# Softmax denominators turned by TensorE, four operand sets in the first unit, finished keys kept in DRAM

## The chip, the cores and the metric

One core of a Trainium2 chip runs the kernel. The metric is the device time of one execution in microseconds (us), median of several runs. TensorE (PE), VectorE (DVE), ScalarE (ACT), GpSimd (POOL) and the queue that issues DMAs (SP) each run their own instruction stream in order.

## The reference

Two batches of eight heads, 768 tokens, head size 64. Each query attends to the keys of its own hash bucket (six sign bits of a projection); then come two feed-forward layers over 1536 tokens, all in fp32:

```python
q_bits = (np.einsum('bhsd,dk->bhsk', q, proj) > 0)      # likewise k_bits; a bucket is the six bits
scores = np.where(q_bucket == k_bucket, q @ k.T / 8, -1e9)
attn = exp(scores - max); attn = attn / (attn.sum(-1) + 1e-9)
x = (attn @ v)                                           # as (1536 tokens, 512)
h = x @ w_in;  x = (s * relu(h)**2 + b) @ w_out          # layer 1: 512 -> 2048 -> 512
h = x @ w_in2; out = (h * clip(h + 3, 0, 6) / 6) @ w_out2  # layer 2
```

## The kernel before

The tokens are cut into four units (two batches, two halves of 384 queries). Attention of a unit goes over four head pairs; pair `g` has six score tiles (two heads, three times 128 queries). A tile is: scores on PE (`qk`, L403), maximum on DVE (`smax`, L409), exponential with its row sum on ACT (`sexp`, L419), six 128x128 transposes on PE (`turn`, L425) and an eviction to SBUF by DVE or ACT (`evict`, L438 and L440). After six tiles `pv_mm` (L462) multiplies with the values. fp32 accuracy comes from splitting operands in a high and a low fp32r part (`k_hi`, `k_lo`, `q_hi`, `q_lo`, L332 to L354); the bucket masks are made by `bits_mm`, `bits`, `code_mm` and `buckets` (L368 to L391) and ride in the low part's other 64 rows.

The row sums stand one per partition, but the product `pv` has the queries along its free axis. So `recip` inverts the six columns, `r_store` (L449) writes them to DRAM element by element, `r_in` (L453) reads them back spread over the partitions as tile `R`, and DVE multiplies (`x_scale`, L467). `x_hi` and `x_lo` split the result for the feed-forward.

The feed-forward is eight jobs (`JOBS`): layer and unit, each 32 weight tiles with 12 matmuls (`mm`, L550), 384 in all. The jobs of units 0 and 1 come first, both layers; the score tiles of the later units are placed between the matmuls. The weights come as 64-bit floats: each tile is loaded (`w_load`, L486), its exponent rebased on ACT (`w_exp`, L494), two 16-bit pieces made (`w_ends`: DVE L503, POOL L506 for the sign and L508 for the rest), joined on DVE (`w_join`, L512), stored (L518), and fetched again by later jobs (`w_fetch`, L522). `w_hi` (ACT) and `w_lo` (POOL, L533) split every weight tile of every job.

The order of all engines is written out ahead of time by a planner (`Plan`): each operation has durations per engine, a due time, operations that it needs, and buffers that it takes and frees. It picks, engine by engine, the one that can start and is due first; where several engines can do an operation, the one that ends it first. The engines then run these lists in order, whatever really happens. The plan holds for the two DMAs of the denominators these lines:

```python
add("DMA", a + 4.0, (0.45, 0.34), r_store, (g,), needs=[("rc", g)], gives=[("rs", g)])
add("DMA", a + 6.5, (0.62, 0.55), r_in, (g,), needs=[("rs", g)], acq=[("R", ("R", g))], gives=[("R", g)])
```

The functions that the change touches:

Of the kernel before, what the change touches and what calls it, by code (L numbers as in the profile page):

```python
# [19 lines left out]
S = 768  # L20
# [8 lines left out]
WARM = 12  # L29
# [5 lines left out]
class Plan:  # L35
# [7 lines left out]

    EPS = {"PE": 0, "ACT": 0.15, "DVE": 0.3, "POOL": 0.15, "SP": 0.3}
# [81 lines left out]
    def forward(self, due):  # L126
# [13 lines left out]
        while left:  # L140
            able = {}
            for o in ready:
# [9 lines left out]
                else:  # L152
                    pick = None
                    for eng, dur in o[0].items():
# [72 lines left out]
def attn_moe_moe2(ctx, tc, qT, kT, vN, cst, w1_in, w1_out, w2_in, w2_out, out):  # L227
# [45 lines left out]
    rden = [dr_p.tile([6, 128], F32, name=f"rd{g}") for g in range(NP)]  # L273
# [6 lines left out]
    def first_unit():  # L280
        p = fab.enter_context(tc.tile_pool(name="first", bufs=1, side="right"))
        K.append([p.tile([128, 2, S], F32R, name=f"K{a}x") for a in range(2)])
        op["kx"] = p
        op["ptx"] = fab.enter_context(tc.tile_pool(name="ptx", bufs=2, side="right"))
        ps["Sx"] = xab.enter_context(tc.tile_pool(name="ps_x", bufs=1, space=PSUM))

    def later_units():
        fab.close()
        p = ctx.enter_context(tc.tile_pool(name="g", bufs=1, side="right"))
        G.extend(p.tile([128, 2, NQ], F32R, name=f"G{f}") for f in range(16))  # L290

# [4 lines left out]
    def keys(g):  # L296
        return K[g % 2 if g < 4 else 0]
# [6 lines left out]

    def load_k(g):
        u, hp = pairs[g]
        if g in (1, 3):
            t = op["kx"].tile([128, 2, S], F32, tag="krx", name="krx")
        else:
            t = one_p.tile([128, 2, S], F32, tag="kr", name="kr")  # L310
        queue[0].dma_start(out=t, in_=kT[units[u][0], hp])
        pd[g]["k"] = t

    def load_q(g):
        u, hp = pairs[g]
# [69 lines left out]
    def buckets(g, nm, h):  # L385
        t = pd[g][nm + "h"][64:128].rearrange("p (i n) -> p i n", i=2)[:, :, 0:384]
        if nm == "k":
            dst = keys(g)[1][64:128, h].rearrange("p (i n) -> p i n", i=2)
            nc.vector.tensor_scalar(out=dst, in0=t, scalar1=cnt, scalar2=-BIG, op0=ALU.not_equal, op1=ALU.mult)
        else:  # L390
            nc.vector.tensor_scalar(out=Q[g % 2][1][64:128], in0=t, scalar1=cnt, scalar2=None, op0=ALU.is_equal)  # L391
# [104 lines left out]
    def w_ends(key, half, on):  # L496
# [8 lines left out]
        elif half:  # L505
            nc.gpsimd.tensor_scalar(out=f16, in0=r16, scalar1=32768.0, scalar2=32768.0, op0=ALU.is_ge, op1=ALU.mult)  # L506
        else:
            nc.gpsimd.tensor_scalar(out=f16, in0=r16, scalar1=2.0 ** -13, scalar2=2.0 ** -14 - 0.5, op0=ALU.mult, op1=ALU.add)  # L508
# [97 lines left out]
    plan = Plan({"S": 2, "Sx": 1, "pv": 1, "mm": 1, "mmx": 2, "P": 2, "pt": 2, "ptx": 2, "v": 2, "R": 1,  # L606
# [31 lines left out]
    add("POOL", A[SPU - 1] + 0.1, 0.0, later_units, (), needs=[("pv", g) for g in range(4)], gives=["G"])  # L638
    for g in range(NP):
# [3 lines left out]
        old = {0: [], 1: [], 2: [0], 3: [1], 4: [2]}.get(g, [g - 1] if g < 9 else [g - 2, g - 1])  # L643
        kfree = [("qk", SPP * x + i) for x in old for i in range(SPP)]
        qfree = [("qk", SPP * (g - 2) + i) for i in range(SPP)] if g > 1 else []
        x = "x" if g in (1, 3) else ""
        St = ("S", "Sx") if g < 4 else "S"
        if own:
            add("DMA", t, (0.62, 2.2), load_k, (g,), acq=[("kr" + x, ("kr", g))], gives=[("k", g)])
            add({"ACT": 1.45, "POOL": 3.0, "DVE": 1.0}, t, 0, k_hi, (g,), needs=kfree + [("k", g)], gives=[("kh", g)], rel=[(("kr", g), 3)])  # L650
            add({"POOL": 3.5, "DVE": 1.7}, t, 0, k_lo, (g,), needs=[("kh", g)], gives=[("kl", g)], rel=[(("kr", g), 3)])
        add("DMA", t, (0.62, 1.1), load_q, (g,), acq=[("qr" + x, ("qr", g))], gives=[("q", g)])
        add({"ACT": 0.75, "POOL": 1.6, "DVE": 0.6}, t, 0, q_hi, (g,), needs=qfree + [("q", g)], gives=[("qh", g)], rel=[(("qr", g), 4)])
        add({"ACT": 0.75, "POOL": 1.6, "DVE": 0.6}, t, 0, q_top, (g,), needs=qfree + [("q", g)], gives=[("qt", g)], rel=[(("qr", g), 4)])
        add({"POOL": 2.9, "DVE": 0.95}, t, 0, q_lo, (g,), needs=[("qh", g)], gives=[("ql", g)], rel=[(("qr", g), 4)])
        for nm in ("kq" if own else "q"):
# [12 lines left out]
        if own or g % 2 == 0 or g < 8:
            pass  # L670
        add("DMA", t + 4, (0.45, 1.1), load_v, (g,), acq=[("v", ("v", g))], gives=[("v", g)])
        for i in range(SPP):
# [4 lines left out]
            add("PE", a, 0.69, qk, (s,), needs=[("kh", gk), ("kl", gk), ("kB", gk, h), ("qt", g), ("ql", g), ("qB", g)] + gate(s) + ([("qk", s - 1)] if s else []),  # L677
                acq=[(St, ("S", s))], gives=[("qk", s)])
            add("DVE", a + 1.0, 0.95, smax, (s,), needs=[("qk", s)], gives=[("mx", s)])
            add("ACT", a + 2.3, 1.17, sexp, (s,), needs=[("mx", s)] + ([("ex", s - 1)] if i else []), acq=[("P", ("P", s))], gives=[("ex", s)])  # L680
            add("PE", a + 3.6, 0.6, turn, (s,), needs=[("ex", s)], gives=[("tr", s)], rel=[(("P", s),)])
            add({"ACT": 0.85, "DVE": 0.85}, a + 4.4, 0, evict, (s,), needs=[("tr", s)] + ([("pt", s - 1)] if tq else []),
                acq=[(("pt", "ptx") if g < 4 else "pt", ("pt", g, h))] if tq == 0 else [], gives=[("pt", s)], rel=[(("S", s),)])
        for c in range(NC):
            add("PE", a + 6.0, 0.64, pv_mm, (g, c),
                needs=[("pv", g, c - 1)] if c else [("pt", SPP * g + i) for i in range(SPP)] + [("v", g)],
                acq=[] if c else [("pv", ("pv", g))], gives=[("pv", g, c) if c < 5 else ("pv", g)],
                rel=[(("pt", g, 0),), (("pt", g, 1),), (("v", g),)] if c == 5 else [])
        add("DVE", a + 3.6, 0.4, recip, (g,), needs=[("ex", SPP * g + i) for i in range(SPP)], gives=[("rc", g)])
        add("DMA", a + 4.0, (0.45, 0.34), r_store, (g,), needs=[("rc", g)], gives=[("rs", g)])  # L690
        add("DMA", a + 6.5, (0.62, 0.55), r_in, (g,), needs=[("rs", g)], acq=[("R", ("R", g))], gives=[("R", g)])
        add("DVE", a + 10.4, 0.6, x_scale, (g,), needs=[("R", g), ("pv", g)], gives=[("xs", g)], rel=[(("R", g),)])
        add("ACT", a + 11.0, 0.48, x_hi, (g,), needs=[("xs", g)], gives=[("xh", g)])
# [121 lines left out]
```

## Time and profile before

| | |
|---|---|
| median of 3 runs | 999.42 us (998.89 to 1007.68) |
| the profiled execution | 1008.91 us, span 1007.1 us |
| busy share of the span | PE 86%, DVE 48%, ACT 49%, POOL 55% |
| matmuls' granted clock, mean | 0.924 |
| DMA | 130.09 MB, mean 129 GB/s |

Busy time is when an engine executes; the ends of matmuls are modelled, so a busy PE is not PE at its peak. The clock is a share of 2.4 GHz. The chain of waits follows the work that ended last back to the start; its shares sum to the span. The profiled execution stands 0.95% above the median; sums are made against it.

### The profile page before, as it was taken

The numbers are of one execution on the slowest core, as the hardware profiler recorded it, in microseconds if no ns is written. First come the engines' busy times: TensorE is split into PE (matmuls) and PEld (weight loads), VectorE is DVE, ScalarE is ACT, GpSimd is POOL, SyncE is SP. The second block draws the span as 40 slices with busy tenths as digits, with TensorE's granted clock in tenths as the row PEclk, the third lists the DMA queues.
The fourth block names the chain that finished last, engine by engine and source line by source line (L and its number), as shares of the span: only waits on it lengthen the run. The fifth ranks groups of instructions, "written<-read, shape, count | busy, mean of one in ns | idle before, by whom it ended". The sixth has DMA issues, their size and how long they took to land.

```text
span 1007.1 us, 13158 instructions
## 1 busy us (share of the span) xinstructions
PE 865.7 (86%) x4668; PEld 718.0 (71%) x4668; DVE 484.8 (48%) x662; ACT 490.1 (49%) x899; POOL 556.9 (55%) x383
## 2 busy tenths in 40 slices
PE   8845569697877999889689889798899899999998
PEld 3523346566465999768466757656799699999998
DVE  6744337576644535788364556243352252250330
ACT  4623246555432654666344646333464374473652
POOL 6733008598665557997664233232364256666664
PEclk7977979899898899999698999898999999999999
DMA  8422324356574347555593355242343244445442
GB/s 300 131 56 55 92 66 157 103 183 145 179 158 109 108 162 231 181 180 166 188 190 97 103 123 86 76 61 79 104 132 95 61 121 131 124 127 149 134 136 85
DMA packets 71601, 130.09 MB, mean 129 GB/s; under 512 B 18672, under 2 KB 26992, under 8 KB 71536
## 3 DMA queue, kind: packets, MB, share of 16 engines
q1 hardware_dynamic: 71392, 129.05, 45.7%
q8 instruction: 36, 0.59, 0.3%
q14 instruction: 29, 0.24, 0.1%
q10 hardware_dynamic: 144, 0.22, 0.1%
HBM read 109.27 MB, written 19.97 MB: 128 GB/s over the span
## 4 chain that ended last, share of the span: by engine, by line
PE 47%; DMA 32%; DVE 8%; POOL 8%; issue 3%; ACT 1%; SPq 1%; DVEq 0%; POOLq 0%; ACTq 0%
PE mm L550 39%; DMA rd<-rs 15%; DMA R<-rd 9%; DMA wr<-w_out 5%; POOL wf L506 4%; PE S L403 3%; PE S L425 2%; DVE wf L512 2%; PE S L368 1%; POOL wl L533 1%; DVE nx L409 1%; POOL wf L508 1%; DMA wr<-w_in 1%; DMA qr<-q_t 1%; PE pv L462 1%
## 5 line engine op out<-in xcount | busy, mean ns | idle before, releaser
L533 POOL TENSOR_TENSOR wl<-wf,wh 128x512 fp32r<-128x512 f32 x256 | 335.9, 1314 | 321.4 <-ACT wh L527 317.9
L550 PE MATMUL mm<-X,wh 128*128 128x384 f32 x1024 | 277.8, 352 | 24.5 <-ACT X L471 19.3
L550 PE MATMUL mm<-G,wh 128*128 128x384 f32 x1024 | 280.1, 355 | 0.0
L527 ACT CAST wh<-wf 128x512 fp32r<-128x512 f32 x256 | 157.8, 617 | 146.7 <-PE mm L550 87.4
L550 PEld LDWEIGHTS mm<-X,wh 128*128 128x128 f32 x1024 | 187.3, 195 | 45.7 <-ACT X L471 20.5
L550 PEld LDWEIGHTS mm<-G,wh 128*128 128x128 f32 x1024 | 185.6, 196 | 33.3 <-issue 30.0
L550 PE MATMUL mm<-G,wl 128*128 128x384 f32 x512 | 177.0, 346 | 7.1 <-POOL wl L533 7.1
L550 PE MATMUL mm<-X,wl 128*128 128x384 f32 x512 | 176.6, 345 | 1.3 <-POOL wl L533 1.3
L403 PE MATMUL S<-K,Q 128*128 128x512 f32 x336 | 82.1, 369 | 49.1 <-DVE ptx L440 24.3
L409 DVE TENSOR_REDUCE nx<-S 128x1 f32<-128x768 f32 x96 | 91.5, 954 | 51.3 <-PE S L403 50.7
L419 ACT ACTIVATE P<-S,nx 128x768 f32<-128x768 f32 x96 | 86.6, 902 | 45.4 <-DVE nx L409 42.5
L550 PEld LDWEIGHTS mm<-G,wl 128*128 128x128 f32 x512 | 100.1, 196 | 8.6 <-POOL wl L533 8.6
L403 PEld LDWEIGHTS S<-K,Q 128*128 128x128 f32 x336 | 58.5, 204 | 66.2 <-DVE pt L440 21.6
L425 PE MATMUL S<-cv,P 128*128 128x128 f32 x576 | 89.5, 298 | 18.8 <-ACT P L419 18.8
L506 POOL TENSOR_SCALAR wf<-wr 128x512 uint16<-128x512 uint16 x45 | 100.7, 2244 | 6.4 <-ACT wr L494 3.3
L425 PEld LDWEIGHTS S<-cv,P 128*128 128x128 f32 x576 | 74.2, 154 | 39.4 <-ACT P L419 23.5
L550 PEld LDWEIGHTS mm<-X,wl 128*128 128x128 f32 x512 | 100.0, 195 | 1.6 <-POOL wl L533 1.6
L512 DVE SCALAR_TENSOR_TENSOR wf<-wr,wf 128x512 int32<-128x512 int32 x64 | 69.7, 1089 | 46.0 <-POOL wf L506 44.8
L508 POOL TENSOR_SCALAR wf<-wr 128x512 uint16<-128x512 uint16 x49 | 47.6, 971 | 60.9 <-DMA wr<-w_out 34.2
L467 DVE TENSOR_TENSOR pv<-pv,R 128x384 f32<-128x384 f32 x16 | 9.0, 566 | 144.1 <-DMA R<-rd 144.1
L494 ACT ACTIVATE wr<-wr 128x512 f32<-128x512 f32 x64 | 43.1, 675 | 68.0 <-DMA wr<-w_out 54.8
L462 PE MATMUL pv<-pt,v 128*64 128x384 f32 x336 | 71.4, 509 | 0.0
(330 smaller groups left out, 777.3 us busy)
## 6 DMA issues: line engine op xcount, KB each, us to landing
wf<-w SPq DMA_DIRECT2D x192, 256.0 KB, 2.7
wr<-w_in SPq DMA_DIRECT2D x32, 512.0 KB, 4.3
w<-wf SPq DMA_DIRECT2D x64, 256.0 KB, 5.6
wr<-w_out SPq DMA_DIRECT2D x32, 512.0 KB, 4.1
kr<-k_t SPq DMA_DIRECT2D x10, 768.0 KB, 4.4
qr<-q_t SPq DMA_DIRECT2D x16, 384.0 KB, 3.9
v<-v_n SPq DMA_DIRECT2D x16, 384.0 KB, 6.8
R<-rd SPq DMA_DIRECT2D x16, 192.0 KB
```

Of the source, the lines that this page charges most:

```text
L403: nc.tensor.matmul(out=sp[:, c0:c1], lhsT=Q[g % 2][a][:, h, 128 * t:128 * t + 128], rhs=keys(g)[a][:, h, c0:c1], start=(a == 0), stop=(a = ...
L409: nc.vector.reduce_max(out=nx, in_=sd[s]["sp"][:, 0:S], axis=AX.X, negate=True)
L419: nc.scalar.activation(out=d["p"], in_=d["sp"][:, 0:S], func=AF.Exp, bias=d["nx"], scale=1.0, accum_out=pd[g]["sums"][:, c:c + 1])
L425: nc.tensor.transpose(d["sp"][:, 128 * c:128 * c + 128], d["p"][:, 128 * c:128 * c + 128], ident)
L462: nc.tensor.matmul(out=d["pv"][64 * h:64 * h + 64, 0:NQ], lhsT=d["v"][:, c, 64 * h:64 * h + 64], rhs=d[h][:, c, :], start=(c == 0), stop=( ...
L494: nc.scalar.activation(out=a, in_=a, func=AF.Copy, scale=2.0 ** -112)
L506: nc.gpsimd.tensor_scalar(out=f16, in0=r16, scalar1=32768.0, scalar2=32768.0, op0=ALU.is_ge, op1=ALU.mult)
L508: nc.gpsimd.tensor_scalar(out=f16, in0=r16, scalar1=2.0 ** -13, scalar2=2.0 ** -14 - 0.5, op0=ALU.mult, op1=ALU.add)
L512: nc.vector.scalar_tensor_tensor(out=wf, in0=wq[key]["raw"][:, :, 1], scalar=3, in1=wf, op0=ALU.logical_shift_left, op1=ALU.bitwise_or)
L527: nc.scalar.copy(hi.rearrange("p a b -> p (a b)"), wq[key]["wf"])
L533: nc.gpsimd.tensor_tensor(out=lo.rearrange("p a b -> p (a b)"), in0=d["wf"], in1=d["hi"].rearrange("p a b -> p (a b)").bitcast(F32), op=AL ...
L550: nc.tensor.matmul(out=a, lhsT=w[:, k, :], rhs=src[k][:, xi, :], start=(k0 + k == 0 and p == 0), stop=(k0 + k == nk - 1 and p == 2))
```

## The change

The denominators no longer go over DRAM. `widen` copies the inverted sums to 64 columns each, `spread` turns the three 128x128 blocks by transposes on PE into PSUM, `r_copy` takes them to SBUF as `R`. For the first four pairs there are four sets of key and query operands in place of two. Their finished keys are stored to DRAM (`k_store`) and fetched (`k_fetch`) for pairs 4 to 7, which share them; these made them anew before. The mask's test is swapped between keys and queries, so that ACT can make the key's (`buckets`). The sign piece of the weights is made on DVE alone, the other also on ACT. Layer 2's weights are converted ahead, from the first matmul of job 1 on, to DRAM, and fetched by job 2 like by the other jobs. The planner has other durations, and adds a weighted duration to an operation's end when it compares engines.

```diff
-WARM = 12
+WARM, PTX, DIRECT = 12, 3, 32
+    WEIGHT = {"DVE": 1.0, "ACT": 0.7}
+                        end += self.WEIGHT.get(eng, 0.0) * (0 if eng == "DMA" else dur)
...
-        K.append([p.tile([128, 2, S], F32R, name=f"K{a}x") for a in range(2)])
+        K.extend([p.tile([128, 2, S], F32R, name=f"K{a}x{e}") for a in range(2)] for e in range(3))
+        Q.extend([p.tile([128, 2, NQ], F32R, name=f"Q{a}x{e}") for a in range(2)] for e in range(2))
...
+    def k_store(g, a):
+        queue[0].dma_start(out=kscr[pairs[g][1]][a], in_=keys(g)[a].bitcast(F32))
+    def k_fetch(g, a):
+        queue[0].dma_start(out=keys(g)[a].bitcast(F32), in_=kscr[pairs[g][1]][a])
...
+        if nm == "q":
+            nc.vector.tensor_scalar(out=queries(g)[1][64:128], in0=t, scalar1=cnt, scalar2=-BIG, op0=ALU.not_equal, op1=ALU.mult)
+            return
+        if on == "ACT":
+            nc.scalar.activation(out=dst, in_=t, func=AF.Relu, bias=below)
...
-    def r_store(g):
-        queue[0].dma_start(out=rden[g].rearrange("s p -> p s"), in_=pd[g]["rs"])
-    def r_in(g):
+    def widen(g, on):
+        rb = one_p.tile([128, QT, 2, 64], F32, tag="rb", name="rb")
+        src = pd[g]["rs"].rearrange("p (h t x) -> p t h x", h=2, x=1).to_broadcast([128, QT, 2, 64])
+        if on == "ACT":
+            nc.scalar.copy(rb, src)
+        else:
+            (nc.gpsimd if on == "POOL" else nc.vector).tensor_copy(out=rb, in_=src)
+    def spread(g):
...
+        for i in range(QT):
+            nc.tensor.transpose(t[:, 128 * i:128 * i + 128], pd[g]["rb"][:, i], ident)
+    def r_copy(g, on):
         R = one_p.tile([128, NQ], F32, tag="R", name="R")
-        queue[0].dma_start(out=R,
-                          in_=rden[g].rearrange("(h x s) p -> h x (s p)", h=2, x=1).to_broadcast([2, 64, NQ]))
+        if on == "ACT":
+            nc.scalar.copy(R, pd[g]["Rp"])
+        else:
+            nc.vector.tensor_copy(out=R, in_=pd[g]["Rp"])
...
-        elif half:
-            nc.gpsimd.tensor_scalar(out=f16, in0=r16, scalar1=32768.0, scalar2=32768.0, op0=ALU.is_ge, op1=ALU.mult)
-        else:
+        elif on == "POOL":
...
+        else:
+            nc.scalar.activation(out=f16, in_=r16, func=AF.Copy, scale=2.0 ** -13, bias=2.0 ** -14 - 0.5)
...
+        if fetched:
+            for x in range(2):
+                add("DMA", t, (0.62, 2.2), k_fetch, (g, x), needs=kfree + [("ks", g - 4, 0), ("ks", g - 4, 1)], gives=[("kh", "kl")[x:x + 1] + (g,)])
...
+                direct = m == 0 and i < DIRECT
+                add("DMA", tw - 4.0, (0.45, 1.46), w_load, (m, i, ck), needs=[("k", 1)] if m == 0 else [("mm", 1, 0)],
```

The new order at three places. DVE in the first unit, from the first pair's reciprocal to its scaling; before (`rs` are the inverted sums, `R` the spread denominators, `nx` a tile's maximum, `wf` a weight tile):

```order
L445 RECIPROCAL rs_520<-rs_520 128x6
L391 TENSOR_SCALAR Q10_114<-S_492,cv_93 64x768
L409 TENSOR_REDUCE nx_535<-S_526 128x1
L409 TENSOR_REDUCE nx_547<-S_537 128x1
L409 TENSOR_REDUCE nx_555<-S_542 128x1
L512 SCALAR_TENSOR_TENSOR wf_385<-wr_364,wf_385 128x512
L467 TENSOR_TENSOR pv_483<-pv_483,R_553 128x384
L440 COPY ptx_583<-S_537 128x6x128
```

and now, the end of that stretch:

```order
L544 SCALAR_TENSOR_TENSOR wf_455<-wr_349,wf_455 128x512
L399 TENSOR_SCALAR Q1x0_189<-S_484,cv_93 64x768
L423 TENSOR_REDUCE nx_566<-S_552 128x1
L423 TENSOR_REDUCE nx_573<-S_561 128x1
L423 TENSOR_REDUCE nx_577<-S_568 128x1
L499 TENSOR_TENSOR pv_491<-pv_491,R_557 128x384
L343 TENSOR_SCALAR Q00_101<-qr_504 128x768
L454 COPY ptx_590<-S_561 128x6x128
```

Five instructions stood between the reciprocal and the multiplication, twelve do now; other work stands behind the multiplication in both.

SP in job 2, where layer 2's weights are loaded (`wr`) and pair 8's denominators go out (`rd`) and come back (`R`); before:

```order
L486 DMA wr_3805<-w2_out 128x1024
L518 DMA w1_19_184<-wf_3732 128x512
L449 DMA rd8_125<-rs_3799 128x6x1
L453 DMA R_3856<-rd8_125 128x1x384
L486 DMA wr_3864<-w2_out 128x1024
L518 DMA w1_20_185<-wf_3763 128x512
```

Of the change, SP in job 1 (`w0_9` is layer 1's tile fetched, `w1_2` layer 2's tile stored, `w2_in` layer 2's source):

```order
L554 DMA wf_2574<-w0_9_122 128x512
L550 DMA w1_2_147<-wf_2551 128x512
L518 DMA wr_2582<-w2_in 128x1024
L518 DMA wr_2589<-w2_in 128x1024
L554 DMA wf_2593<-w0_10_123 128x512
L550 DMA w1_3_148<-wf_2567 128x512
```

Layer 2's loads and stores moved from job 2 into job 1, and no load stands behind a transfer of denominators.

SP in the first unit of the change (`ks` are the kept keys, `K0` and `K1` the operands of pair 4 on, `kr` raw keys):

```order
L550 DMA w0_0_113<-wf_295 128x512
L327 DMA ks02_109<-K0x1_184 128x1536
L330 DMA K1_100<-ks10_106 128x1536
L330 DMA K0_99<-ks00_105 128x1536
L327 DMA ks03_111<-K0x2_186 128x1536
L317 DMA kr_432<-k_t 128x1536
```

Stores of finished keys and the fetches of pair 4 now stand between the loads.

## Rows read from the trace of the kernel before

**Rows 1.** The page: chain that ended last, by engine and by line.
```profile
PE 47%; DMA 32%; DVE 8%; POOL 8%; issue 3%; ACT 1%; SPq 1%; DVEq 0%; POOLq 0%; ACTq 0%
PE mm L550 39%; DMA rd<-rs 15%; DMA R<-rd 9%; DMA wr<-w_out 5%; POOL wf L506 4%; PE S L403 3%; PE S L425 2%; DVE wf L512 2%; PE S L368 1%; POOL wl L533 1%; DVE nx L409 1%; POOL wf L508 1%; DMA wr<-w_in 1%; DMA qr<-q_t 1%; PE pv L462 1%
```
**Rows 2.** Waits of DVE, whole span: us in total, times, longest us.
```profile
DVE pv L467 <- DMA R<-rd: 144.1, 14, 16.1
```
**Rows 3.** Waits of the SP queue, whole span.
```profile
SPq L453 <- DMA rd<-rs: 143.9, 16, 11.7
SPq L486 <- DVE wf L512: 130.0, 42, 9.2
```
**Rows 4.** Chain in order of time, in job 2: start us, us, what.
```profile
505.03 0.70 PE S L403 x4
...
510.48 12.18 DMA rd<-rs
...
523.87 9.44 DMA wr<-w_out
...
551.67 7.50 DMA R<-rd
```
**Rows 5.** Windows, first unit, jobs 0-4: us, busy (PE PEld DVE ACT POOL), PEclk, DMA.
```profile
0.00:147.00 147.00, 95.40 (x481) 55.10 (x481) 75.41 (x95) 56.00 (x96) 57.65 (x32) 0.82 0.39 119
147.00:327.00 180.00, 144.52 (x746) 108.45 (x746) 112.20 (x138) 87.06 (x159) 130.60 (x81) 0.90 0.54 145
327.00:398.00 71.00, 70.90 (x391) 68.29 (x392) 34.05 (x50) 39.12 (x75) 42.99 (x34) 0.96 0.51 160
398.00:560.00 162.00, 136.44 (x703) 107.76 (x701) 100.58 (x130) 81.97 (x153) 117.47 (x78) 0.89 0.61 173
560.00:715.00 155.00, 133.63 (x732) 102.04 (x732) 71.66 (x101) 71.56 (x133) 45.92 (x33) 0.94 0.39 83
715.00:804.00 89.00, 85.18 (x476) 77.04 (x477) 32.66 (x50) 46.66 (x88) 41.33 (x33) 0.98 0.35 100
```
**Rows 6.** Waits of DVE in the first unit (0:147), then in job 3 (560:715).
```profile
DVE pv L467 <- DMA R<-rd: 46.0, 4, 13.9
...
DVE pv L467 <- DMA R<-rd: 41.5, 4, 16.1
```
**Rows 7.** Timeline, first unit, PE and its weight loads (PEld): start, us, instructions.
```profile
47.42 1.29 PEld L425 LDWEIGHTS S<-cv,P 128*128 128x128 f32 x12 [0.60 <-ACT P L419]
...
68.93 0.83 PE L368 MATMUL S<-qr,cv 64*32 64x384 f32 x4
...
106.12 2.16 PE L462 MATMUL pv<-pt,v 128*64 128x384 f32 x12
```
**Rows 8.** Chain in order of time, jobs 5 to 7.
```profile
803.83 199.81 PE mm L550 x1142
```
**Rows 9.** Groups by shape: count, busy us, mean ns, idle before.
```profile
L512 DVE SCALAR_TENSOR_TENSOR wf<-wr,wf 128x512 int32<-128x512 int32 x64 | 69.7, 1089 | 46.0 <-POOL wf L506 44.8
L440 DVE COPY pt<-S 128x768 f32<-128x768 f32 x35 | 33.4, 954 | 23.5 <-PE S L425 22.4 <-ACT wh L527 0.9
L503 DVE TENSOR_SCALAR wf<-wr 128x512 uint16<-128x512 uint16 x34 | 29.1, 867 | 17.4 <-DMA wr<-w_out 10.6 <-POOL wl L533 4.6 <-DMA wr<-w_in 1.9
L389 DVE TENSOR_SCALAR K<-S,cv 64x768 fp32r<-64x768 f32 x20 | 20.5, 1024 | 4.6 <-PE S L382 4.2
L506 POOL TENSOR_SCALAR wf<-wr 128x512 uint16<-128x512 uint16 x45 | 100.7, 2244 | 6.4 <-ACT wr L494 3.3 <-DVE mm L567 0.2
L533 POOL TENSOR_TENSOR wl<-wf,wh 128x512 fp32r<-128x512 f32 x256 | 335.9, 1314 | 321.4 <-ACT wh L527 317.9 <-PE mm L550 1.1
```
**Rows 10.** One line's instructions, L503: ns min/median/max, first and last start.
```profile
L503 DVE TENSOR_SCALAR wf<-wr x34: 450/790/2051, 151.8 to 535.1; 128x512 uint16<-128x512 uint16 x34
```
**Rows 11.** The page: DMA issues, KB each, median us to landing.
```profile
kr<-k_t SPq DMA_DIRECT2D x10, 768.0 KB, 4.4
```
**Rows 12.** Windows, the first 20 us: columns as in Rows 5.
```profile
0.00:20.00 20.00, 15.90 (x59) 6.39 (x60) 12.09 (x16) 8.63 (x12) 11.90 (x10) 0.80 0.88 332
```

More of the change, by code (lines that the diff above doesn't have):

```diff
@@ L290, in later_units @@
         G.extend(p.tile([128, 2, NQ], F32R, name=f"G{f}") for f in range(16))
+        X.extend([p.tile([128, 2, NQ], F32R, name=f"X{e}{k}") for k in range(4)] for e in range(1, 4))
     def mm_banks():
@@ L642, in attn_moe_moe2 @@
         own = new_keys(g)
[L643 to L646, printed above, removed]
+        old = [g - 1] if 4 < g < 9 else [g - 2, g - 1] if g > 8 else [0] if g == 4 else []
+        kfree = [("qk", SPP * x + i) for x in old for i in range(SPP)] + ([("ks", 0, 0), ("ks", 0, 1)] if g == 4 else [])
@@ L647, in attn_moe_moe2 @@
+        qfree = [("qk", SPP * (g % 2 if g in (4, 5) else g - 2) + i) for i in range(SPP)] if g > 3 else []
         St = ("S", "Sx") if g < 4 else "S"
[L648 to L656, printed above, removed]
+        fetched = 4 <= g < 8
@@ new lines, in attn_moe_moe2 @@
+        if fetched:
+            for x in range(2):
+                add("DMA", t, (0.62, 2.2), k_fetch, (g, x), needs=kfree + [("ks", g - 4, 0), ("ks", g - 4, 1)], gives=[("kh", "kl")[x:x + 1] + (g,)])
+        elif own:
+            add("DMA", t, (0.62, 2.2), load_k, (g,), acq=[(("kr", "krx") if g < 4 else "kr", ("kr", g))], gives=[("k", g)])
+            add({"ACT": 1.5, "POOL": 4.1, "DVE": 1.3}, t, 0, k_hi, (g,), needs=kfree + [("k", g)], gives=[("kh", g)], rel=[(("kr", g), 3)])
+            add({"POOL": 3.7, "DVE": 2.0}, t, 0, k_lo, (g,), needs=[("kh", g)], gives=[("kl", g)], rel=[(("kr", g), 3)])
+            if g < 4:
+                for x in range(2):
+                    add("DMA", t + 20.0, (0.62, 2.2), k_store, (g, x), needs=[("kl", g), ("kB", g), ("kB", g, 0)] if x else [("kh", g)], gives=[("ks", g, x)])
@@ new lines, in attn_moe_moe2 @@
+        add("DMA", t, (0.62, 1.1), load_q, (g,), acq=[(("qr", "qrx") if g < 4 else "qr", ("qr", g))], gives=[("q", g)])
+        add({"ACT": 0.84, "POOL": 2.6, "DVE": 0.7}, t, 0, q_hi, (g,), needs=qfree + [("q", g)], gives=[("qh", g)], rel=[(("qr", g), 4)])
+        add({"ACT": 0.84, "POOL": 2.4, "DVE": 0.7}, t, 0, q_top, (g,), needs=qfree + [("q", g)], gives=[("qt", g)], rel=[(("qr", g), 4)])
+        add({"POOL": 4.0, "DVE": 1.22}, t, 0, q_lo, (g,), needs=[("qh", g)], gives=[("ql", g)], rel=[(("qr", g), 4)])
@@ L657, in attn_moe_moe2 @@
+        for nm in ("kq" if own and not fetched else "q"):
             nh = 2 if nm == "k" else 1
             key = ("h", nm, g)
-            add("PE", t, 0.74, bits_mm, (g, nm), needs=(kfree if nm == "k" else qfree) + [(nm, g)], acq=[(St, key)],
+            add("PE", t, 0.85, bits_mm, (g, nm), needs=(kfree if nm == "k" else qfree) + [(nm, g)], acq=[(St, key)],
                 gives=[(nm + "m", g)], rel=[((nm + "r", g), 3 if nm == "k" else 4)])
-            add("DVE", t, 0.6, bits, (g, nm), needs=[(nm + "m", g)], acq=[("bt", ("bt", nm, g))], gives=[(nm + "b", g)])
+            add("DVE", t, 0.56, bits, (g, nm), needs=[(nm + "m", g)], acq=[("bt", ("bt", nm, g))], gives=[(nm + "b", g)])
@@ L689, in attn_moe_moe2 @@
[L689 to L693, printed above, removed]
+        add("PE", a + 6.0, 4.2, pv_mm, (g,), needs=[("pt", SPP * g + i) for i in range(SPP)] + [("v", g)],
+            acq=[("pv", ("pv", g))], gives=[("pv", g)], rel=[(("pt", g, 0),), (("pt", g, 1),), (("v", g),)])
@@ new lines, in attn_moe_moe2 @@
+        add("DVE", a + 3.6, 0.58, recip, (g,), needs=[("ex", SPP * g + i) for i in range(SPP)], gives=[("rc", g)])
+        add({"ACT": 0.5, "POOL": 1.2, "DVE": 0.5}, a + 4.5, 0, widen, (g,), needs=[("rc", g)], acq=[("rb", ("rb", g))], gives=[("rb", g)])
+        add("PE", a + 6.5, 0.4, spread, (g,), needs=[("rb", g)], acq=[("mm" if g < 4 else "S", ("R", g))], gives=[("Rp", g)], rel=[(("rb", g),)])
+        add({"ACT": 0.48, "DVE": 0.55}, a + 7.5, 0, r_copy, (g,), needs=[("Rp", g)], acq=[("Rs", ("Rs", g))], gives=[("R", g)], rel=[(("R", g),)])
@@ L694, in attn_moe_moe2 @@
+        add("DVE", a + 10.4, 0.6, x_scale, (g,), needs=[("R", g), ("pv", g)], gives=[("xs", g)], rel=[(("Rs", g),)])
+        add("ACT", a + 11.0, 0.48, x_hi, (g,), needs=[("xs", g)] + (["G"] if u else []), gives=[("xh", g)])
         add("DVE", a + 11.5, 0.55, x_lo, (g,), needs=[("xh", g)], gives=[("x", u, hp)], rel=[(("pv", g),)])
```

118 lines of the change are left out of this document (57 added, 61 removed).

## The prediction, made before the changed kernel ran

> **What bounds the kernel now.** I read the chain of waits on the page first. There the reader sees that 24% of the span, some 240 us, lies in two transfers, the denominators' way out (`rd<-rs`, 15%) and back (`R<-rd`, 9%), and another 5% in loads of weights [rows 1]. Then the waits by engine: DVE stands idle for 144.1 us in 14 waits before `x_scale`, each time for `R` [rows 2]. DVE runs in order, so the maxima and evictions behind it wait too. The queue that issues DMAs pays a second time: the read waits for the write's landing, 143.9 us in 16 times [rows 3], and every load behind it waits as well. Job 2 shows it: 12.18 us for the write to land, then 9.44 us for a weight load that had stood behind it [rows 4]. Last I read the windows by stage [rows 5]. PE is busy in 86% of the span, yet the stages with score tiles are much longer than their matmuls. Jobs 5 to 7, which have no tiles, run 1142 matmuls in 199.81 us, 0.175 us each [rows 8], so 384 take 67.2 us. PE's other prices: a tile's scores 0.70 us [rows 4], its six transposes half of 1.29, 0.645; a pair's values 24 records, of which 12 took 2.16, so 4.2 at most; four small mask matmuls 0.83 [rows 7].
>
> Job 3 tells whether other losses are large. By the order it held 23 tiles' scores and transposes, four pairs' values and 28 mask matmuls: 67.2 + 16.1 + 14.8 + 16.8 + 5.9 = 121 us of PE. It took 155 [rows 5], with 41.5 us of DVE waiting for `R` [rows 6]. So nearly all of its loss is that wait.
>
> **The change, part by part.** The round trip goes: 12.18 + 7.50 us where job 2's rows show it [rows 4]. Instead there are a copy of 128x384, three transposes and another copy. The trace has no `widen`. Its bounds are half of DVE's 0.954 us for 128x768, 0.5, and POOL's 2.24 us for 512 elements [rows 9]; three transposes are half of 0.645, 0.3. With the second copy at 0.5 the way takes 1.3 to 3.1 us; I take 2.5 with the handoffs, since most copies go to ACT and DVE. By the order twelve DVE instructions stand between reciprocal and multiplication, five before; at about 0.9 us each, they cover 2.5 us. So I cost the wait at nothing; if these twelve were done early, each of 16 pairs would pay up to 3. The queue's 143.9 us go with it.
>
> The time then depends on what is late next. I sum by stage: what the changed order puts there, by the rows' durations, against the engine or resource that has most.
>
> *First unit.* It took 147 us: DVE busy 75.4 [rows 5], 46.0 for `R` [rows 6], the rest start and refills. DVE now has ten key masks fewer (to ACT, 1.024 each) and four evictions fewer (0.954), but seven sign pieces more (0.867 [rows 9]), net four more scalings of queries and keys (at the eviction's 0.954), and five short copies (0.5): -10.2 - 3.8 + 6.1 + 3.8 + 2.5 = -1.6. So 147 - 46.0 - 1.6 = 99. Four operand sets let masks and splits run ahead of the tiles, and there is less refilling: I take **97**. Less than the busy time and the first 20 us' idle, 73.8 + 7.9 [rows 12] = 82, it can't be. Eight stores of 768 KB are new, 6.3 MB; with all else some 20 MB go in this stage, 60 us at the 332 GB/s of [rows 12], under its 97.
>
> *Job 0.* PE has 21 tiles' scores, 22 of transposes, four pairs' values, 24 mask matmuls, four spreads: 67.2 + 14.7 + 14.2 + 16.8 + 5.0 + 1.3 = 119. POOL, busy 130.6 before [rows 5], loses its sign pieces, 45 of 2.244 us in jobs 0 and 2 [rows 9]: about 22 here, 49 us, and under half of the other pieces too. DVE gains 15 pieces (13.0) and loses six masks, seven evictions and four key splits (about -19): 106. All stay under 119 but near it, and an order fixed ahead can't fill every hole. I take **127**, for 180. Fetching kept keys moves two times 768 KB after a pair's last scores; one lands in 4.4 us [rows 11], two by some 7, while the order puts 15, 12 and 45 matmuls, twelve transposes and mostly a pair's values there, 7.3 to 9.2 us. So it is covered, barely; without the cover three pairs would cost 7 each, 21.
>
> *Job 1.* Empty of tiles before, 71 us [rows 5]; now it has ten tiles and all of layer 2's conversion. PE: 67.2 + 7.0 + 5.2 + 4.2 + 1 = 85. DVE's 32 pieces and joins alone are 32 x (0.867 + 1.089) [rows 9] = 63 beside the 34 it had and some 13 for tiles, 110. DMA: 32 loads of 512 KB, 32 stores and 32 fetches of 256 KB and 2 MB more make 35.6 MB, 107 us at 332 GB/s [rows 12] or 113 at this job's own 160 GB/s for a 0.51 share [rows 5]. I take **116**: a stage that grows by 45, and gives job 2 what it takes.
>
> *Job 2.* Conversion and denominators leave it. PE: 67.2 + 10.5 + 10.3 + 12.6 + 5.5 + 0.6 = 107; with 3% for holes **111**, for 162. *Job 3:* 17 and 18 tiles, three pairs: 67.2 + 11.9 + 11.6 + 12.6 + 3.8 + 1.3 = 108, **112** for 155. *Job 4:* six tiles, 67.2 + 4.2 + 3.9 + 4.2 + 1.1 = 81, **84** for 89. *Jobs 5 to 7* stay at **203**, the span's 1007 less 804.
>
> Sum: 97 + 127 + 116 + 111 + 112 + 84 + 203 = 850. The profiled execution stood 1.8 us above its span: 852. It was 1008.91 against a median of 999.42, so on the median's scale 852 / 1.0095 = **844 us**.
>
> **Weighed against the skill.** DVE's sign piece, 16-bit in and out of SBUF, took 450 ns at best, 790 in the median and 2051 at worst [rows 10]; the mean of 867 prices it above. The Trainium skill, SBUF — State Buffer, Who interferes with whom, says that VectorE in a two-port mode, or with two SBUF inputs, and GpSimd lock each other out for a whole instruction. The spread from 450 to 2051 agrees with such a lock, and this change puts more of these instructions on DVE beside POOL's splits.
>
> **The rivals.**
> 1. *Every stage at its bound*: 82 + 119 + 107 + 107 + 108 + 81 + 203 + 2 = 809, **801** on the median's scale. For it: job 3 lost little but the wait. Against: four engines near full in job 0.
> 2. *DVE and POOL hold each other up* in jobs 0 and 1. If each of DVE's 57 sign pieces there waits out one POOL split, it takes 1.314 [rows 9] + 0.450 [rows 10] = 1.76 in place of 0.867: 51 us more, 903, **894**. This is the skill's rule at its worst; against it, the mean of 867 was already taken beside a POOL busy in 73% of jobs 0 and 2.
> 3. *A new wait takes the old one's place*: `x_scale` still stands in order ahead of evictions, and `r_copy` comes after exponentials on ACT. At half of the old wait per pair, 144.1 / 16 / 2 = 4.5, it is 72 us: 924, **915**.
> 4. *Slower*: the queue stalls on the sixteen stores and fetches of kept keys as it did on the denominators. If each held the loads behind it as long as the write in job 2 did, 12.18 us, it is 195 us: 1047, **1037**. It decides from (1019 - 852) / 16 = 10.4 us each. Against it: the load of the same size landed in 4.4 us [rows 11], and a store has no one waiting right behind it but the fetch far later.
> 5. *It doesn't do what it says*: PE was busy 86%, and if that were work and not matmuls stretched by a mean clock of 0.82 to 0.94 in the stages with tiles [rows 5], the waits would be hidden and the time stay near **999**. Against: 0.175 us a matmul at clock 1.00.
>
> **The numbers.** Chances: the forecast 0.60 (by itself 820 to 885), rival 1 0.14, rival 2 0.12, rival 3 0.09, rival 4 0.02, rival 5 0.03. The range goes from 795, a little under rival 1, to 905, over rival 2; about 0.05 lies under it and 0.14 above. A measurement of this kernel tells about 1% from no change, 989 to 1009 here. Faster 0.95, same 0.03, slower 0.02.
>
> **What would show it.** DVE's waits should hold no line of `x_scale` over 20 us in total, and the chain no transfer of denominators. The first matmul of job 0 should stand near 97, job 1 near 116 us with a DMA share above 0.8, job 2 near 111 with POOL busy under 60 us. I am wrong if `x_scale` waits for `R` over 60 us, if scores wait for fetched keys, if job 1 passes 130 us, or if DVE's sign piece takes over 1.2 us on the mean.

## The result, and the profile of the changed kernel

The changed kernel takes **870.74 us** (median of 4 runs, 867.29 to 874.40), the kernel before 1003.39 beside it (998.89 to 1007.68): a ratio of **0.868 [0.862, 0.874]**. The forecast was 844, its range 795 to 905. The profiled execution took 870.84 us, 868.7 of them the span.

First the page's chain, by engine and by line, which answers to [rows 1]:

```profile
PE 73%; DMA 11%; DVE 7%; ACT 5%; issue 2%; POOL 1%; SPq 0%; DVEq 0%; ACTq 0%; POOLq 0%
PE mm L582 52%; PE S L417 6%; PE pv L494 6%; PE S L439 6%; DMA w<-wf 3%; DMA wr<-w_out 2%; DMA wr<-w_in 2%; DVE wf L544 2%; DVE wf L535 2%; DMA wf<-w 2%; ACT P L433 1%; PE S L379 1%; DVE nx L423 1%; PE S L393 1%; DVE Q L343 1%
```

The two transfers of denominators, 24% before, are gone. PE has gone from 47% of the chain to 73%. Among the transfers that are left, one that is not in the list of [rows 1] leads: `w<-wf`, the store of a converted piece of weights. PE's busy time fell as well, from 865.7 us to 819.5 with 4668 matmul records in both, while the mean granted clock rose from 0.924 to 0.969. So of the 138 us by which the span is shorter, 92 are idle time of PE that is gone, and 46 are PE's matmuls, the same number, taking less.

Second the windows by stage, cut at the first matmul of jobs 0, 1, 2, 3, 4 and 5 (columns as in [rows 5]):

```profile
0.00:101.30 101.30, 84.41 (x463) 49.41 (x463) 75.37 (x94) 65.61 (x107) 34.03 (x23) 0.93 0.62 232
101.30:231.40 130.10, 125.80 (x747) 104.44 (x745) 103.78 (x138) 93.73 (x173) 88.20 (x63) 0.99 0.68 219
231.40:357.50 126.10, 103.65 (x512) 93.09 (x512) 83.09 (x118) 74.22 (x136) 69.16 (x59) 0.86 0.80 268
357.50:471.20 113.70, 111.50 (x656) 93.71 (x655) 52.22 (x74) 72.94 (x130) 49.73 (x36) 0.98 0.40 120
471.20:582.40 111.20, 111.20 (x671) 95.78 (x670) 49.74 (x76) 70.83 (x130) 46.49 (x35) 1.00 0.32 99
582.40:664.00 81.60, 81.60 (x480) 76.79 (x479) 30.80 (x48) 47.71 (x89) 41.15 (x32) 1.00 0.37 106
664.00:868.70 204.70, 201.36 (x1153) 201.04 (x1152) 58.77 (x102) 108.84 (x204) 121.21 (x94) 1.00 0.43 125
```

Outside the first unit and job 1, PE is busy in all but 2 to 4 us of a stage, or in all of it. The stage that stands out is job 1: 126 us, PE busy in 104 of them at a granted clock of 0.86, no engine full, the DMA engines at 0.80. The 71 us that [rows 5] give it before start 7 us behind its first matmul; cut as here, it took 77.7 us, with PE busy in 72.3:

```profile
320.00:397.70 77.70, 72.34 (x399) 69.41 (x399) 34.31 (x51) 39.34 (x74) 42.77 (x33) 0.96 0.52 162
```

The cuts of [rows 5] at 560, 715 and 804 us lie some 6 us late in the same way, so jobs 5 to 7 took 209 us before, not 203; ahead of the one at 147 stand nine early matmuls of job 0.

Third the waits of DVE for `x_scale`, which answer to [rows 2], and windows over the three longest of them:

```profile
DVE pv L499 <- ACT R L484: 46.7, 6, 10.1
```
```profile
221.50:230.60 9.10, 9.10 (x46) 5.40 (x43) 0.05 (x1) 2.06 (x4) 0.85 (x1) 0.81 0.22 73
571.70:581.60 9.90, 9.90 (x62) 7.21 (x61) 0.04 (x2) 2.52 (x4) 3.38 (x3) 1.00 0.34 101
653.00:663.10 10.10, 10.10 (x61) 7.43 (x60) 0.07 (x1) 2.90 (x5) 3.35 (x3) 1.00 0.20 55
```

DVE still stands idle for 46.7 us here, but in those 29.1 us PE is busy in 29.1, and in the other three waits, 17.7 us, it is busy throughout as well. Before, PE was busy in 80.9 of the 144.1 us of [rows 2]. The second window, by instructions (start, us, engine, line):

```profile
571.16 0.55 DVE L469 COPY rb<-rs 128x384 f32<-128x384 f32 x1
581.57 0.57 DVE L499 TENSOR_TENSOR pv<-pv,R 128x384 f32<-128x384 f32 x1 [9.86 <-ACT R L484]
```
```profile
580.35 0.34 PE L582 MATMUL mm<-G,wl 128*128 128x384 f32 x1
580.53 0.49 PE L478 MATMUL S<-cv,rb 128*128 128x128 f32 x3
580.77 0.59 PE L582 MATMUL mm<-G,wh 128*128 128x384 f32 x2
```

The widened denominators are ready at 571.7. PE turns them at 580.5, since values and weight matmuls stand ahead in its order. DVE waits because PE is full, and PE is the engine that bounds the stage: such a wait costs nothing here.

Last the SP queue's waits in job 1:

```profile
SPq L554 <- DMA w<-wf: 35.9, 15, 5.0
SPq L550 <- DVE wf L544: 21.5, 15, 5.3
SPq L554 <- POOL wl L565: 17.3, 8, 3.5
```

The first is the pattern of the round trip at another place. A fetch of weights (L554) takes the buffer from which a converted piece is being stored, so it cannot be issued until that store has landed, and every load behind it waits too.

### The profile page after: what moved, and what is told of

Read it like the earlier page. It is cut to its first block, busy times and chain, and to the rows that moved or that the text cites. A ratio compares the mean times of both kernels' runs of the same rounds, so it can differ in the third digit from the quotient of the medians.

```text
span 868.7 us, 13213 instructions
## 1 busy us (share of the span) xinstructions
PE 819.5 (94%) x4668; PEld 714.3 (82%) x4668; DVE 453.8 (52%) x649; ACT 533.9 (61%) x965; POOL 450.0 (52%) x341
## 2 busy tenths in 40 slices
DMA packets 63313, 144.72 MB, mean 167 GB/s; under 512 B 6800, under 2 KB 13072, under 8 KB 63248
## 4 chain that ended last, share of the span: by engine, by line
PE 73%; DMA 11%; DVE 7%; ACT 5%; issue 2%; POOL 1%; SPq 0%; DVEq 0%; ACTq 0%; POOLq 0%
PE mm L582 52%; PE S L417 6%; PE pv L494 6%; PE S L439 6%; DMA w<-wf 3%; DMA wr<-w_out 2%; DMA wr<-w_in 2%; DVE wf L544 2%; DVE wf L535 2%; DMA wf<-w 2%; ACT P L433 1%; PE S L379 1%; DVE nx L423 1%; PE S L393 1%; DVE Q L343 1%
## 5 line engine op out<-in xcount | busy, mean ns | idle before, releaser
L582 PE MATMUL mm<-X,wh 128*128 128x384 f32 x1024 | 270.5, 346 | 10.5 <-DVE G L614 10.5
L582 PE MATMUL mm<-G,wh 128*128 128x384 f32 x1024 | 273.5, 349 | 0.7 <-ACT wh L559 0.7
L582 PEld LDWEIGHTS mm<-X,wh 128*128 128x128 f32 x1024 | 184.4, 191 | 18.6 <-DVE G L614 12.3
L439 PE MATMUL S<-cv,P 128*128 128x128 f32 x576 | 83.3, 283 | 9.5 <-ACT P L433 9.4
L452 ACT COPY pt<-S 128x768 f32<-128x768 f32 x79 | 63.1, 801 | 27.0 <-PE S L439 26.8
L417 PE MATMUL S<-K,Q 128*128 128x512 f32 (+1 forms) x312 | 70.5, 353 | 0.6 <-ACT pt L452 0.5
L538 POOL TENSOR_SCALAR wf<-wr 128x512 uint16<-128x512 uint16 x53 | 46.9, 886 | 37.8 <-DMA wr<-w_in 14.2
L494 PE MATMUL pv<-pt,v 128*64 128x384 f32 x336 | 63.2, 502 | 0.0
L544 DVE SCALAR_TENSOR_TENSOR wf<-wr,wf 128x512 int32<-128x512 int32 x64 | 56.8, 888 | 7.8 <-POOL wf L538 2.6
L417 PEld LDWEIGHTS S<-K,Q 128*128 128x128 f32 x312 | 53.1, 197 | 8.5 <-issue 2.6
L535 DVE TENSOR_SCALAR wf<-wr 128x512 uint16<-128x512 uint16 x64 | 51.2, 803 | 16.0 <-ACT wr L526 9.2
```

Source lines behind the costliest of these rows:

```text
L417: nc.tensor.matmul(out=sp[:, c0:c1], lhsT=queries(g)[a][:, h, 128 * t:128 * t + 128], rhs=keys(g)[a][:, h, c0:c1], start=(a == 0), stop=(a ...
L439: nc.tensor.transpose(d["sp"][:, 128 * c:128 * c + 128], d["p"][:, 128 * c:128 * c + 128], ident)
L452: nc.scalar.copy(dst, src)
L535: nc.vector.tensor_scalar(out=f16, in0=r16, scalar1=(13, 0x8000)[half], scalar2=None, op0=(ALU.logical_shift_right, ALU.bitwise_and)[half])
L544: nc.vector.scalar_tensor_tensor(out=wf, in0=wq[key]["raw"][:, :, 1], scalar=3, in1=wf, op0=ALU.logical_shift_left, op1=ALU.bitwise_or)
L582: nc.tensor.matmul(out=a, lhsT=w[:, k, :], rhs=src[k][:, xi, :], start=(k0 + k == 0 and p == 0), stop=(k0 + k == nk - 1 and p == 2))
```

## The experiments

Each kernel was timed in rounds with the kernel before on the same chip. Differences between two experiments are those of their ratios, times 1003 us. Edits are to the changed kernel, unless said; each is shown by its main lines, with `...` for what is left out. With an edit the planner writes a new order, so an experiment compares two whole plans.

**1. The denominators' way, undone and alone.** In the first experiment's kernel all else of the change stays and the denominators go over DRAM again, with the old planned durations.

```
-    add({"ACT": 0.5, ...}, a + 4.5, 0, widen, ...); spread; r_copy
+    add("DMA", a + 4.0, (0.45, 0.34), r_store, (g,), needs=[("rc", g)], gives=[("rs", g)])
+    add("DMA", a + 6.5, (0.62, 0.55), r_in, (g,), needs=[("rs", g)], acq=[("R", ("R", g))], ...)
```

> The changed kernel with one part undone: the denominators go over DRAM again, planned with the old durations. Theory A (the round trip, as a wait of VectorE and of the DMA queue, was most of what the change took away): 955 us, 930 to 1000, and VectorE waits for R over 80 us. Theory B (the waits were mostly hidden; moved conversions and operand sets made the gain): under 895 us.

Measured: a ratio of 1.003 [0.998, 1.008], some 1005 us. Theory A's direction held, but more came back than its range allowed: everything. The old waits are there again, now L482 and L468:

```profile
DVE pv L482 <- DMA R<-rd: 163.7, 14, 17.0
...
SPq L468 <- DMA rd<-rs: 137.6, 16, 13.7
```

The second experiment's kernel is the one before with `widen`, `spread` and `r_copy` in place of `r_store` and `r_in`, and nothing else of the change.

> The kernel before with this part alone: denominators widened, turned on TensorE, copied. Theory A: 915 us, 885 to 945. Theory B: 970 us or more. With both e1 and e2 the parts can be seen to add up (the sum of the two differences near 133 us) or to overlap.

Measured: 877.7 us, ratio 0.879 [0.873, 0.884], better than theory A's range. So this part alone is worth 121 of the 132 us, and without it the rest together, in that plan with its short transfers, is worth nothing.

**2. Was it the landing time, or a plan that did not know of it?** The kernel before, its denominators still over DRAM; only the planner's idea of when such a transfer has landed is changed, so that it orders other work between.

```
                 clock["DMA"] = end = start + dur[1]
+                end += {"r_store": 8.5, "r_in": 6.0}.get(fn.__name__, 0.0)
```

> The kernel before, denominators over DRAM, but the planner is told that the store is done 8.5 us and the read 6.0 us later than it believed (about what the trace shows), so that it puts other work ahead of the multiplication and of the read. Theory A1 (the cost was a plan that believed in a short round trip): VectorE's wait for R falls under 50 us and the time to 940 us, 900 to 965. Theory A2 (the latency itself costs: one PSUM bank and the order of the queue are held for it whatever is planned): 975 us or more.

Measured: 931.5 us, ratio 0.932 [0.927, 0.938]: theory A1. DVE's waits for `R`, 144.1 us before [rows 2], are 7.0:

```profile
DVE pv L468 <- DMA R<-rd: 7.0, 2, 5.4
```

With the same transfers and engines, a true duration in the plan is worth 68 us, over half of what removing the transfers is worth. How the remaining 54 us are made up (`pv`'s one buffer that is held longer, or the many small packets in the DMA engines) was not separated.

**3. Layer 2's conversion, ahead in job 1 or in line in job 2.**

```
-                direct = m == 0 and i < DIRECT
+                direct = i < DIRECT
-                add("DMA", tw - 4.0, ..., w_load, ..., needs=[("k", 1)] if m == 0 else [("mm", 1, 0)],
+                add("DMA", tw - 4.0, ..., w_load, ..., needs=[("k", 1)] if m == 0 else past(jn, i, AHEAD),
```

> The changed kernel, but layer 2's weights are converted in job 2 as they are used, not ahead in job 1. Theory C: job 1 falls from 126 to 90 us, job 2 grows from 114 to 145, sum 860 to 880. Theory D (converting ahead is part of the gain): 885 us or more.

Measured: **832.1 us**, ratio 0.831 [0.827, 0.835]: 37 us faster than the changed kernel, and below what either theory gave. Windows of its jobs 1, 2 and 3:

```profile
231.60:314.80 83.20, 83.20 (x490) 78.28 (x489) 39.68 (x60) 54.63 (x101) 45.66 (x37) 1.00 0.49 152
314.80:425.70 110.90, 107.72 (x639) 92.14 (x638) 94.79 (x125) 90.02 (x166) 83.62 (x62) 1.00 0.71 227
425.70:543.00 117.30, 117.30 (x711) 99.23 (x709) 48.80 (x74) 76.64 (x139) 47.66 (x35) 1.00 0.34 103
```

Job 1 loses 42.9 us. Job 2 takes the whole conversion, DVE going from 52.2 us busy to 94.8, and gets 2.8 us *shorter*; job 3 grows by 6.1. The conversion fits beside job 2's tiles and matmuls, and there a converted piece is used from the buffer it was made in. Ahead, each of 32 pieces has to be fetched again for job 2: the page counts 224 fetches of weights for 192 and 144.72 MB for 136.33. The number of stores is the same, 64, since later jobs fetch from them either way; but ahead, layer 2's stores share four buffers with the fetches of layer 1 for job 1.

**4. What makes job 1 long when it converts.** Three edits of the changed kernel: half of the conversion loaded only behind job 1's last matmul, so that it runs beside job 2; five buffers for converted weights in place of four; no stores of layer 2, whose later fetches then read layer 1's pieces.

```
-                ..., needs=[("k", 1)] if m == 0 else [("mm", 1, 0)],
+                ..., needs=[("k", 1)] if m == 0 else [("mm", 1, 0 if i < 16 else 31)],
```

> The changed kernel, but the second half of layer 2's weights (16 tiles) is loaded for conversion only after the last matmul of job 1, so that it runs beside job 2's first half. Job 2 uses 120 GB/s and TensorE bounds it. If job 1 is overfull with traffic and job 2 has room: job 1 100 us (95 to 110), job 2 117, sum 850 (842 to 862). If the conversion costs as much wherever it stands: 866 to 880.

```
-WR_BUFS, WF_BUFS, AHEAD = 3, 4, 8
+WR_BUFS, WF_BUFS, AHEAD = 3, 5, 8
```

> The changed kernel with five buffers for converted and fetched weight tiles in place of four. In job 1 the queue waits 36 us for stores to land before a fetch may have its buffer. If buffers make job 1's 126 us: job 1 115 or less, 858 us. If the bytes do (33.6 MB at 267 GB/s, DMA engines 80% busy): job 1 122 to 128, 866 to 873 us.

```
         w = wdone.pop(key)
+        if m == 0:
             queue[0].dma_start(out=wscr[m][i], in_=w)
...
-        queue[0].dma_start(out=wf, in_=wscr[m][i])
+        queue[0].dma_start(out=wf, in_=wscr[0][i])
```

> The changed kernel, where layer 2's converted pieces are not stored to DRAM and the later fetches of layer 2 read layer 1's stored pieces in their place (so layer 2 is computed with wrong weights). Job 1 keeps all its conversions on DVE, ACT and POOL, in the same order; 32 stores, 8.4 of its 33.6 MB, and the hold that a store has on its buffer are gone. Theory A, job 1's length is set by transfers and by buffers that wait for a store to land (35.9 us in 15 waits of the queue): job 1 falls from 126 to 95 to 105, the kernel takes 841 to 852. Theory B, DVE's and ACT's conversion work itself sets it (DVE busy 83.1 of 126): job 1 stays at 118 or more, the kernel takes 862 to 871.

Half later: 869.2 us, 0.868 [0.864, 0.873]. Loaded ahead, it costs the same beside either job: job 1 falls to 98.0 and job 2 rises to 136.3. Five buffers: 859.1, 0.857 [0.853, 0.861], 11 us less. No stores: 851.5, 0.851 [0.848, 0.855], 17 us less, as theory A had it for the time; its job 1 of 108.9 is a little over A's 95 to 105. Job 1 with five buffers, then without stores:

```profile
234.30:346.40 112.10, 97.21 (x519) 87.95 (x517) 77.16 (x113) 71.11 (x133) 71.30 (x60) 0.92 0.84 283
```
```profile
234.10:343.00 108.90, 93.83 (x512) 83.41 (x511) 87.76 (x118) 73.29 (x136) 68.93 (x59) 0.97 0.70 236
```

With a fifth buffer job 1 was 14 us shorter and moved 283 GB/s for 268 (31.7 MB for 33.8), and the queue's wait for a store to land fell from 35.9 us to 12.6:

```profile
SPq L554 <- DMA w<-wf: 12.6, 6, 4.2
```

So job 1 was not at the limit of the DMA engines: with them busier, it got shorter. The buffers that a store holds until it has landed are worth the 11 us that a fifth buffer gives; the 17 us without stores count the bytes of the stores too, and the two were not separated further. The other 26, from 109 to the 83 of the in-line kernel, belong to the rest of the conversion; which of its steps sets them was not isolated.

**5. The other parts.** The sign piece back on POOL (with it ACT makes none of the other pieces, and the plan has its old durations, 1.0 us for a piece on POOL); the first batch's keys made anew for the second unit instead of fetched, and not stored; then both in the in-line kernel, and in that kernel the planner's weights of DVE and ACT taken out.

```
-                add("DVE", tw, 0.85, w_ends, (ck, 1), ...)
+                add({"POOL": 1.0, "DVE": 0.71}, tw, 0, w_ends, (ck, 1), ...)
```

> The changed kernel with the weights' pieces as before: sign piece on GpSimd or VectorE, the other not on ScalarE, old durations. If GpSimd's 2.24 us sign pieces were part of the bound of the conversion, jobs 0 and 1 get longer and the time is 885 us, 875 to 905. If VectorE and GpSimd locking each other out is what now limits jobs 0 and 1, it gets no longer or shorter: 855 to 872.

```
-        fetched = 4 <= g < 8
+        fetched = False
```

> The changed kernel, but no keys are stored or fetched: pairs 4 to 7 load and split their keys and make their masks again, as before. Theory C (with the round trip gone, the other parts only move time between stages): 865 to 880 us, job 0 longer by under 10 us, the first unit shorter by 0 to 3. Theory D (kept keys are part of the gain): 885 us or more, job 0 longer by 15 or more.

> The changed kernel with layer 2 in line (832.1 us), the sign pieces given back to POOL and the first batch's keys made anew for the second unit. Theory A, the two parts are worth what they were worth in the changed kernel, 15.4 and 12.9 us: 855 to 865. Theory B, they were worth that only since job 1 was over-full: 832 to 845. Theory C, they hang together (keys made anew load POOL and DVE just where the sign pieces stand): over 868, near the 878 of the denominators' new way alone.

```
-    WEIGHT = {"DVE": 1.0, "ACT": 0.7}
+    WEIGHT = {}
```

> The changed kernel with layer 2 in line (832.1 us), and the planner's table WEIGHT emptied, which makes it charge DVE and ACT more than POOL when it chooses an engine. Theory A, the weighting is what the other parts gained (in-line version 832 against 878 with the denominators' new way alone): 845 or more. Theory B, it only moves copies between engines that both have room: 828 to 838.

Sign on POOL: 886.2, 0.889 [0.883, 0.895], 21 us slower than the changed kernel, as the first theory had it. Keys anew: 883.7, 0.881 [0.877, 0.886], 13 slower, between the two figures expected; job 0 grew by 9.7 us, as theory C had it. Both in the in-line kernel: 886.2, 0.885 [0.882, 0.888], 54 slower than 832.1, theory C. Its job 0 is 150.9 and its job 2 140.6 us long, for 129.9 and 110.9. Two groups of that run show the sign pieces, and the joins that wait for them (L538 is POOL's sign piece here, in the changed kernel its other piece):

```profile
L538 POOL TENSOR_SCALAR wf<-wr 128x512 uint16<-128x512 uint16 x52 | 116.1, 2239 | 7.2 <-ACT wr L526 4.0
L544 DVE SCALAR_TENSOR_TENSOR wf<-wr,wf 128x512 int32<-128x512 int32 x64 | 70.7, 1106 | 47.0 <-POOL wf L538 44.3 <-DMA w<-wf 2.0 <-POOL wf L540 0.2
```

It is the same picture as before the change, 44.8 us of waiting behind a piece of 2244 ns [rows 9]; in the changed kernel the joins wait 2.6 us for POOL. How the 54 us divide was not tried by itself, but 30 of them are in job 2, where none of the second unit's keys are made, so the sign pieces seem to have the larger part. Whether that is the piece or the plan, which counts 1.0 us for its 2.24, is open: experiment 2 shows what a wrong duration can cost, and the sign piece on POOL was not tried with its true one. These 886.2 us are not under the 877.7 of the denominators' new way alone, so what is left of the change (four operand sets, the swapped mask, the other durations) gains nothing that can be told. Without the weights: 836.6, 0.835 [0.832, 0.838], theory B: no difference that can be told.

**6. A better version.** The in-line kernel, and in it a fifth buffer.

> The changed kernel with layer 2 converted in line in job 2 (832.1 us) and, besides, five buffers of converted weights for four. Theory A, the buffers matter only where stores and fetches of weights share them in one stage: that stage is now job 2, which took 111 us with 107.7 of them PE's own, so at most 3 are to be had: 828 to 834. Theory B, the eleven microseconds that a fifth buffer gave with the conversion ahead (870.7 to 859.1) come again, since 32 conversions still share the buffers with 32 pieces in jobs 0 and 2: 818 to 825.

Measured: 833.3 us, 0.833 [0.830, 0.835]. Theory A: with layer 2's stores out of job 1, the fifth buffer is worth nothing. The best kernel of this study is the changed one with layer 2 in line, 832.1 us, 17% under the kernel before.

## Why the prediction was right, and where it was not

**The main step held.** The round trip was read as the bound, its removal priced through the stages, and the first unit, jobs 0, 2, 3, 4 and 5 to 7 came at 101, 130, 114, 111, 82 and 205 for 97, 127, 111, 112, 84 and 203. The instructions of the new way were priced well too: `widen` took 0.50 to 0.55 us in the median, three transposes 0.49, the second copy 0.48 or 0.56, together 1.5.

**The handoffs, and why the wait costs nothing, were not right.** The way was taken at 2.5 us, covered by twelve DVE instructions. From the reciprocal's end to `R` it took 1.8 to 18.6 us, 10.7 in the median, because the transposes stand behind other work in PE's order: between the 16 widened copies and their first transposes lie 139.5 us, with PE busy in 135.0. Twelve is the first pair's count; at the six pairs that wait, one to ten instructions stand there, and the waits reach 10.1 us where the prediction allowed up to 3. From the reciprocal's end to the multiplication it is still 13.7 us in the median, for 17.9 before. The term of nothing came true for another reason than the one given, and that was luck: the new way waits only while PE has other work, while the old one waited whether PE had work or not.

**The 27 us by which 844 was low** have three parts. Job 1 is 10 of them, the other stages 9. The remaining 8 are the step from the profiled scale to the median's: 852 / 1.0095 carried over how the profiled execution before stood to its median, and this kernel's profiled execution stood at its median.

**The mis-sized term is job 1**, "a stage that grows by 45, and gives job 2 what it takes". Its size came from DVE at 110 or the DMA engines at 107 to 113. It measured 126, with DVE busy for 83 and the DMA engines 0.80: neither limit was reached. What was missing is, in part, the hold of a buffer until its store has landed: job 1 was 14 us shorter with a fifth buffer, and 17 without the stores. The second half of the sentence is wrong as well. Job 2 was not long because it held the conversion: with the whole conversion in it, it takes 110.9 us. It was long through the round trip and through joins that wait for POOL's sign pieces: cut at its first matmul it took 156.4 us before and 135.4 with the denominators' new way alone, and 28.2 of the 44.8 us of [rows 9] lie in it. I had counted that piece in POOL's busy time, and never as a wait of DVE. So the change has a part that loses 37 us, inside a sum that was right because my 111 for job 2 holds either way.

**A mark I set was wrong.** "No line of `x_scale` over 20 us" was missed, with 46.7, yet the wait cost nothing, PE being busy in all of it. The mark should have been PE's idle time, not DVE's. None of the signs of being wrong came true, though job 1's 126 us came near the 130: `x_scale` did not wait 60 us, no row of PE's waits has scores waiting for a fetched key, and DVE's sign piece took 803 ns on the mean.

**The rivals.** *Every stage at its bound*, 801: not reached, though the in-line kernel shows that 832 was there. (Its 107 for job 1 lies under the 110 that the prediction itself counts for DVE in it.) *DVE and POOL hold each other up*, 894, asked for 1.76 us of every sign piece; here is that line (ns min/median/max):

```profile
L535 DVE TENSOR_SCALAR wf<-wr x64: 444/552/1668, 19.7 to 352.2; 128x512 uint16<-128x512 uint16 x64
```

Its mean is 803 ns, and the trace tells what it is made of. The 22 pieces that started with POOL idle took 445 to 467 ns. The 42 that started beside an instruction of POOL took 985 ns on the mean, and 36 of these ended 0.31 to 0.38 us after that instruction's end, as here:

```profile
339.23 1.67 POOL L565 TENSOR_TENSOR wl<-wf,wh 128x512 fp32r<-128x512 f32 x1 [5.39 <-ACT wh L559]
339.68 1.53 DVE L535 TENSOR_SCALAR wf<-wr 128x512 uint16<-128x512 uint16 x1
```

The Trainium skill, SBUF — State Buffer, Who interferes with whom, describes a lock of VectorE and GpSimd for a whole instruction; this trace agrees. So the rival's mechanism is there and lifts the mean from 456 to 803 ns, by estimate 22 us of DVE over 64 pieces. But only 14 of the 64 took over 1.2 us, and DVE was not full in jobs 0 and 1: busy for 104 of 130 us and for 83 of 126. *A new wait in the old one's place*, 915: the wait is there, without its price. *Slower*, 1037, by a queue that stalls on kept keys: a fetch landed in 6.3 us, under the 10.4 from which it decides, and keeping keys gains 13 us. The queue did stall on stores, 35.9 us, but on those of weights, where I had not looked. *No effect*, 999: no; of the span's 138 us, 92 are idle time of PE. The other 46 are the stretched matmuls of which this rival speaks: the granted clock is 0.98 to 1.00 in jobs 0, 2 and 3 now, for 0.89 to 0.94, and it rose when the waits went.

## What to carry to other kernels

When work is moved to a stage that looks empty, ask first whether it was in the way where it stood, and count what the move itself adds: here 32 fetches, and buffers that are held until a store has landed. A transfer whose result is waited for has to stand in a plan with its landing time, since an in-order queue and an in-order engine both pay for an optimistic one: 68 us here for one line. Judge a wait by whether the bounding engine is idle in it: PE was busy in 81 of the 144 us before, and in all 47 after.

## What the runs showed of the hardware that was not expected

POOL's time for one shape depends on the operations: 128x512 16-bit elements took 2244 ns with a comparison and a multiplication [rows 9], and 886 ns with a multiplication and an addition (971 in the kernel before). Here is the second, and below it the same piece made on ACT:

```profile
L538 POOL TENSOR_SCALAR wf<-wr 128x512 uint16<-128x512 uint16 x53 | 46.9, 886 | 37.8 <-DMA wr<-w_in 14.2 <-DMA wr<-w_out 8.6 <-DMA w<-wf 6.8
L540 ACT ACTIVATE wf<-wr 128x512 uint16<-128x512 uint16 x11 | 8.6, 785 | 3.4 <-DMA wr<-w_out 3.4
```

The denominators' transfers were small in bytes and large in packets. The page's packet lines of the kernel before and of the one with only that part changed:

```profile
DMA packets 71601, 130.09 MB, mean 129 GB/s; under 512 B 18672, under 2 KB 26992, under 8 KB 71536
```
```profile
DMA packets 56977, 126.90 MB, mean 144 GB/s; under 512 B 6096, under 2 KB 12368, under 8 KB 56912
```

By the difference, 16 round trips were 14,624 packets, 914 each, 786 of them under 512 bytes, for 3 KB of denominators; the stores among them landed after up to 12.18 us [rows 4].
